# First MoE matmul of the last three batches: seven half-size products and Silu, in place of plain tiles with tanh and a gate

## The chip, the cores and the metric

The kernel runs on one core of one Trainium2 chip. The metric is the device time of one execution in microseconds (us). Three runs of the kernel before took 525.06, 526.71 and 526.99 us; the median is 526.71 us. The profile belongs to the run of 525.06 us, and its span is 523.3 us.

## The reference

```python
scores = q @ k.transpose(0, 1, 3, 2) / np.sqrt(64)        # batch 8, 12 heads, 448 tokens, head 64
attn = softmax(scores)                                    # over the last axis
x = (attn @ v).transpose(0, 2, 1, 3).reshape(3584, 768)
h = x @ w_in                                              # w_in 768 x 2048
g = h * (1 / (1 + np.exp(-h)))                            # silu
out = g @ w_out                                           # w_out 2048 x 768, out float32
```

## The kernel before, in words

The eight batches b0 to b7 go through four kinds of work.

**Attention.** Twelve heads are taken four at a time, so a batch has three units (b0 has six, because its queries come in two pieces). DVE turns K and Q (lines 362 and 373), PE computes the scores (L383) into PSUM tiles p_0 and p_1, ACT takes the exponential of 896 columns at a time (L408), PE multiplies the exponentials with a block of ones and with V (L432), and DVE transposes and inverts the sums (L454 to L459) and writes the normalized x to the tiles xT (L465).

**First MoE matmul.** The class `Plain` (L1206 and below) makes one of the sixteen 128-wide slices f of h for one batch: six matmuls of 128x448 with w_in (L485) into one PSUM bank, a tanh on ACT (L498), and a gate on DVE (L501) that computes (tanh + 1) * x and writes G, and in b1 and b5 partly X. xT holds half of the value of x, so that this is silu. There are four buffers for the tanh.

**Second MoE matmul.** The class `Quad` (L753; its matmuls are L804) takes two token tiles of 128 and computes their product with w_out by seven block products in place of eight. The sums of G that it needs are made on DVE and POOL (L510, tiles S, and E when attention needs no more of those), the sums of w_out are in the tiles TO, and the adds behind the products read PSUM on DVE (L510, tiles t and p). Copies out of PSUM go to ACT (L514) or DVE (L516), and stores go out on SP's queue (L545).

**Sums of w_in.** `plan_w_in_sums` makes the sums SI1, SI2 and SI4 of blocks of w_in on DVE and POOL, and one more in place in w_in_t, which has to wait for the last plain batch. In the kernel before nothing reads them.

**What sets the order.** The kernel builds its own order. A planner, the class `Order` and the loop at the end, keeps a clock for PE, ACT, DVE and POOL with an assumed price for each operation, and always emits what could start first by that clock. An engine then runs its instructions in the order in which they were emitted. So the planner's prices move no data; they decide which instruction stands behind which. Eight PSUM banks are handed out in four tiles p_0 to p_3 of two banks each; p_0 and p_1 belong to the scores and are lent to the other work when there are no scores to do (`lent`).

**The other path for the first matmul.** The class `Fold` (L862 to L1031; its matmuls are L920) is in the kernel and is not reached when PLAIN is 8. It makes two slices of h, f and f + 8, at once by seven products of three matmuls of 128x224 in the order 1, 5, 2, 6, 7, 3, 4. A copy of 448 columns out of PSUM follows product 5 (ACT or DVE), the adds y, c22, c12 and c21 of 224 columns run on DVE with one operand in PSUM, the subtraction z runs on POOL. From batch SILU on, each of the two results is then one Silu on ACT (L506) that writes G. `plan_t` adds four sums of xT per batch on DVE (tile T, 672 columns, and one in place in xT). While more than QB (4) of a batch's Silu are open, no scores are started (`silu_phase`), and ACT keeps the Silu table (`loose`).

```python
            elif m == 6:
                add("y", "DVE", y, A[:, n : 2 * n], p1, ALU.add, [op])
                add("z", ZENG, p5, y, p5, ALU.subtract, [ev["y"]])
...
            elif m == 3:
                c12 = add("c12", "DVE", A[:, n : 2 * n], A[:, n : 2 * n], p1, ALU.add, [op])
                self.finish(A[:, 0 : 2 * n], self.f, [c12], True)
            elif m == 4:
...
                c21 = add("c21", "DVE", p5, Bq, p5, ALU.add, [op, ev["z"]], lambda at: banks.give(k, at))
                self.finish(F[:, 1:3].rearrange("p i n -> p (i n)"), self.f + HF, [c21], False)
            if m in (6, 7) and self.at >= 5 and "c22" not in ev:
                Bq = bank(self.banks[1])[:, 0:n]
                add("c22", "DVE", y, Bq, y, ALU.add, [self.last7, ev["y"]] + [ev["z"]])
```

Of the kernel before, what the change touches and what calls it, by code (L numbers as in the profile page):

```python
# [200 lines left out]
def kernel(  # L201
# [34 lines left out]
    LIM_H = 3  # L236
    LIM_E, LIM_S, LEND = 2, 2, 1
    LONE = NG + 1
    PLAIN = 8
    SILU = 8  # L240
    HIGH = 'POOL'
    ZENG = 'POOL'
    PIECES = ((0, 7), (7, TPP))
# [231 lines left out]
    def g_parts(b, t0, t1):  # L475
        cut = 6 * 128 - S if b % 4 == 1 else S
        r = b % 2
        for lo, hi, dst, at in ((0, cut, G, S * r), (cut, S, X, -cut)):
            lo, hi = max(lo, t0), min(hi, t1)
            if lo < hi:  # L480
                yield lo - t0, hi - t0, dst, at + lo
# [179 lines left out]
    def plan_turns(upto):  # L661

        while turned["n"] < min(upto, NU):
            if not plan_turn(turned["n"]):
                return
            turned["n"] += 1
# [49 lines left out]
    def plan_w_in_sums():  # L716
        for f in range(HF):
# [8 lines left out]
            def used(f=f):  # L726
                made = []
                for b in range(PLAIN):
                    got = plain_ops.get((b, f + HF), [])
# [132 lines left out]
    class Fold:  # L862
# [36 lines left out]
        def room(self):  # L899
            m = self.step()  # L900
            if m == 1:
                at = [x for x in (f_slots.when(1), e_slots.when(1)) if x is not None]
                return [min(at) if at else None]
            if m in (3, 4) and self.b < SILU:
                return [th_slots.when(1)]
# [23 lines left out]
        def run(self):  # L929
            m, n, ev = self.step(), S // 2, self.ev  # L930
            self.at += 1
            if m == 1:
                self.borrow = not f_slots.can(1, od.now)
                self.fi = (e_slots if self.borrow else f_slots).take(od.now)
                if self.b >= SILU and self.b not in silu_left:
                    silu_left[self.b] = NFF * len(list(g_parts(self.b, 0, S)))
# [43 lines left out]
        def finish(self, src, ff, deps, psum):  # L980
# [8 lines left out]

            if b < SILU:  # L990
                ti = th_slots.take(od.now)
# [43 lines left out]
    def plan_t(b):  # L1035

        if b in t_op or not all((b, c, 0) in x_op for c in range(NDC)):
            return
        if not T_slots.can(1, od.now):
            return  # L1040
        T_slots.take(od.now)
        n = S // 2
        x = {
            (h, t): x_s[x_at[(b, h)]][:, :, n * t : n * (t + 1)] for h in range(2) for t in range(2)
        }
        ops = [[x_op[(b, c, 0)] for c in range(HC * h, HC * (h + 1))] for h in range(2)]

        def sums(out, u, w, deps):
            return od.add(
                Op("DVE", half(HC * n), lambda: tt(out, u, w, ALU.subtract), deps, SLOW + 2)  # L1050
            )

        o1 = sums(T_s[:, 0], x[0, 1], x[0, 0], ops[0])
        o2 = sums(T_s[:, 1], x[1, 1], T_s[:, 0], [o1] + ops[1])
        o4 = sums(T_s[:, 2], x[1, 0], T_s[:, 1], [o2])
        o3 = sums(x[0, 1], x[1, 1], x[0, 1], [o1] + ops[1])
        t_op[b] = {1: o1, 2: o2, 3: o3, 4: o4}
# [14 lines left out]
    def s_place():  # L1072
        if s_slots.can(1, od.now):
            return "S", s_slots.take(od.now)
        if not qk_seq and not av_seq and len(t_op) == B - PLAIN and e_slots.can(1, od.now):
            return "E", e_slots.take(od.now)
# [185 lines left out]
    for b in range(B):  # L1262
        if b >= PLAIN:
            moe += [Fold(b, f) for f in range(HF)]
# [327 lines left out]
    while True:  # L1592
        plan_turns(qk_seq[0][0][0] + 3 if qk_seq else NU)
        for b in range(PLAIN, B):
            plan_t(b)
# [73 lines left out]
```

## Time and profile before

| what | us |
|---|---|
| three runs | 525.06, 526.71, 526.99 |
| the profiled run, its span | 525.06, 523.3 |
| PE busy | 428.2 (82%) |
| DVE busy | 281.6 (54%) |
| ACT busy | 235.6 (45%) |
| POOL busy | 210.6 (40%) |
| first matmul of b5 on PE | 359.8 to 384.3, and 4 of its 96 matmuls at 348.6 |
| first matmul of b6 on PE | 420.5 to 443.4, and 6 matmuls at 413.9 |
| first matmul of b7 on PE | 470.2 to 489.5, and 6 matmuls between 462.6 and 464.8 |
| last scores of the kernel on PE | 394.7 |

A row of the profile names the source line, the engine, the tiles written and read, the shape, the count, the busy time and the mean of one, and the idle time before with what ended it. The timeline gives the same with start times counted from the start of the span. The windows give each engine's busy time in a stretch. A matmul's end is modelled, so that PE's busy time holds a piece behind each group of matmuls in which only the last results drain.

### The profile page before, as it was taken

Reading aid. Unit: us, or ns where it says so; the run is one execution under the profiler, and the core shown is the slowest. Engines: PE = TensorE matmul, PEld = TensorE weight load, DVE = VectorE, ACT = ScalarE, POOL = GpSimd, SP = SyncE. Lnnn points to the kernel's source line nnn. Section 1 sums busy time; section 2 is a strip of 40 time slices with the busy share of each in tenths; the row PEclk is TensorE's granted clock in tenths of the full one; section 3 lists DMA queues with packets and bytes.
Section 4 is the critical chain, followed back from the end, with each engine's and each line's share of the span. In section 5 each row is a group of like instructions: output and inputs, shape, how many; then the busy total and the mean of one; then the engine's idle time right before and its main releaser. Section 6 shows DMA issues by size and latency. Waiting matters only on the chain.

```text
span 523.3 us, 9760 instructions
## 1 busy us (share of the span) xinstructions
PE 428.2 (82%) x3853; PEld 210.9 (40%) x3853; DVE 281.6 (54%) x565; ACT 235.6 (45%) x356; POOL 210.6 (40%) x277
## 2 busy tenths in 40 slices
PE   8997787977589879888788987798788777779775
PEld 7655443332244334333333433343333433444332
DVE  2455866768756644663357534665466234624721
ACT  3876567767016564554236643457341123114210
POOL 5667969758542510851019510453033000302500
PEclk9999989999699999999999999999999999999989
DMA  8898065997043630653107520073000210021022
GB/s 117 113 183 135 2 85 77 186 169 112 1 76 85 92 75 1 77 97 79 31 1 98 105 75 5 8 115 63 3 1 22 58 41 1 16 76 31 0 54 69
DMA packets 38750, 34.46 MB, mean 66 GB/s; under 512 B 11952, under 2 KB 37936, under 8 KB 38704
## 3 DMA queue, kind: packets, MB, share of 16 engines
q0 software_dynamic: 27952, 22.82, 31.4%
q1 hardware_dynamic: 9984, 10.24, 7.2%
q10 hardware_dynamic: 768, 0.79, 0.6%
q8 instruction: 30, 0.49, 0.4%
q14 instruction: 16, 0.13, 0.1%
HBM read 45.61 MB, written 11.01 MB: 108 GB/s over the span
## 4 chain that ended last, share of the span: by engine, by line
PE 53%; DVE 17%; DMA 10%; ACT 8%; issue 7%; POOL 4%; DVEq 0%; ACTq 0%; POOLq 0%
PE p L485 22%; PE p L804 21%; PE p L432 7%; ACT th L498 6%; DMA rq<-in_q_dram 5%; DVE G L501 4%; PE p L383 3%; DMA w_in_t<-in_moe_w_in_dram 2%; DVE xT L465 2%; DVE t L510 2%; DVE S L510 2%; DVE E L510 2%; DMA rk<-in_k_dram 2%; DVE t L454 2%; POOL V L329 2%
## 5 line engine op out<-in xcount | busy, mean ns | idle before, releaser
L485 PE MATMUL p<-xT,w_in_t 128*128 128x448 f16 (+1 forms) x864 | 164.3, 333 | 37.3 <-ACT th L498 18.1
L408 ACT ACTIVATE E<-p 128x896 f16<-128x896 f32 (+1 forms) x172 | 148.6, 916 | 73.1 <-PE p L383 72.2
L501 DVE SCALAR_TENSOR_TENSOR G<-th,p 128x448 f16<-128x448 f16 (+2 forms) x144 | 76.3, 535 | 104.1 <-ACT th L498 47.7
L485 PEld LDWEIGHTS <-w_in_t 128*128 128x128 f16 x864 | 82.4, 98 | 117.8 <-issue 61.0
L498 ACT ACTIVATE th<-p 128x448 f16<-128x448 f32 (+1 forms) x144 | 70.5, 502 | 109.1 <-PE p L485 47.2
L804 PE MATMUL p<-w_out_t,G 128*128 128x384 f16 x304 | 61.4, 333 | 14.1 <-DVE t L510 6.8
L510 POOL TENSOR_TENSOR G<-G 128x512 f16<-128x512 f16 x21 | 25.1, 1206 | 95.5 <-DVE S L510 95.0
L514 ACT COPY t<-p 128x384 f32<-128x384 f32 x39 | 18.5, 478 | 99.6 <-PE p L804 79.4
L804 PEld LDWEIGHTS <-G 128*128 128x128 f16 x416 | 39.2, 99 | 57.1 <-issue 35.2
L383 PE MATMUL p<-QT,KT 32*128 32x448 f16 (+4 forms) x864 | 55.9, 342 | 2.3 <-ACT E L408 2.2
L329 POOL DMA_DIRECT2D V<-in_v_dram x88 | 48.9, 563 | 14.8 <-PE p L432 11.2
L432 PE MATMUL p<-E,V 128*32 128x448 f16 (+2 forms) x864 | 44.5, 337 | 8.0 <-DVE X L501 6.0
L804 PE MATMUL p<-TO,S 128*128 128x384 f16 x192 | 40.9, 340 | 12.1 <-DVE t L454 4.3
L510 DVE TENSOR_TENSOR t<-p,t 128x384 f32<-128x384 f32 x42 | 23.3, 554 | 49.4 <-PE p L804 46.4
L510 POOL TENSOR_TENSOR E<-E,E 128x896 f16<-128x896 f16 x18 | 35.5, 1971 | 31.9 <-ACT E L408 31.7
L804 PEld LDWEIGHTS <-S 128*128 128x128 f16 x280 | 26.0, 99 | 44.5 <-issue 29.2
L465 DVE SCALAR_TENSOR_TENSOR xT<-p,t 128x448 f16<-128x448 f32 (+1 forms) x54 | 30.2, 566 | 18.3 <-PE p L432 15.1
L432 PEld LDWEIGHTS <-V 128*32 128x32 f16 (+1 forms) x864 | 20.4, 96 | 28.8 <-issue 18.3
L510 POOL TENSOR_TENSOR G<-X,G 128x512 f16<-128x512 f16 x4 | 4.9, 1214 | 62.4 <-DVE S L510 62.4
L383 PEld LDWEIGHTS <-KT 32*128 32x128 f16 (+2 forms) x864 | 17.3, 98 | 29.9 <-issue 28.3
L454 DVE STREAM_TRANSPOSE t<-p 128x448 f32<-128x448 f32 (+1 forms) x27 | 16.0, 594 | 20.7 <-PE p L432 10.5
L804 PE MATMUL p<-TO,G 128*128 128x384 f16 x112 | 21.8, 326 | 4.3 <-ACT t L514 3.5
(60 smaller groups left out, 347.3 us busy)
## 6 DMA issues: line engine op xcount, KB each, us to landing
out_dram<-t SPq DMA_DIRECT2D x208, 48.0 KB, 1.6
rk<-in_k_dram POOLq DMA_DIRECT2D x24, 224.0 KB, 4.7
rq<-in_q_dram POOLq DMA_DIRECT2D x21, 224.0 KB, 5.2
w_out_t<-in_moe_w_out_dram POOLq DMA_DIRECT2D x8, 384.0 KB, 7.8
V<-in_v_dram POOLq DMA_DIRECT2D x43, 64.0 KB, 2.8
V<-in_v_dram POOLq DMA_DIRECT2D x40, 48.0 KB, 2.5
w_in_t<-in_moe_w_in_dram POOLq DMA_DIRECT2D x16, 96.0 KB, 4.6
w_in_t<-in_moe_w_in_dram POOLq DMA_DIRECT2D x8, 192.0 KB, 8.4
```

The lines of the kernel that those rows point to most:

```text
L329: nc.gpsimd.dma_start(out=V[32 * x : 32 * (x + 1), hs, 0:count, :], in_=v[b, hs].rearrange("h (i g) d -> i h g d", g=TPP)[:, :, first : fi ...
L383: nc.tensor.matmul(out=P_s[s_pair][p0 : p0 + 32 * (x1 - x0), h % 2, at : at + nq], lhsT=KT[(b, hg)][32 * h : 32 * (h + 1), c, x0:x1, :, e] ...
L408: nc.scalar.activation(out=E_s[e_i][0:kr, 2 * y : 2 * y + 2, 0:nk], in_=P_s[s_pair][0:kr, :, 0:nk], func=AF.Exp, scale=attn_scale,)
L432: nc.tensor.matmul(out=bank(a)[32 * h : 32 * (h + 1), 0:nq], lhsT=w, rhs=E_s[sum_at[n] if part == 0 and c in sums else es[c // per_burst(n)]][
L454: nc.vector.transpose(out=t, in_=grouped(n, bank(a)))
L465: nc.vector.scalar_tensor_tensor(out=x_s[xi][:, cc % HC, 32 * g0 : 32 * g1], in0=bank(a)[:, 0:nq], scalar=0.5, in1=t_s[ti][:, 0:nq], op0=A ...
L485: nc.tensor.matmul(out=bank(a)[:, 0 : t1 - t0], lhsT=w_in_t[:, cc, 128 * f : 128 * (f + 1)], rhs=x_s[x_at[(b, cc // HC)]][:, cc % HC, t0:t ...
L498: nc.scalar.activation(out=th, in_=src, func=AF.Tanh)
L501: (nc.vector if eng == "DVE" else nc.gpsimd).scalar_tensor_tensor(out=out, in0=th, scalar=1.0, in1=x, op0=ALU.add, op1=ALU.mult)
L510: e.tensor_tensor(out=out, in0=a, in1=b, op=op)
L514: nc.scalar.copy(out=out, in_=in_)
L804: nc.tensor.matmul(out=bank(a)[:, 0 : self.n], lhsT=lhs(i), rhs=rhs(i), start=(start and i == 0), stop=(i == last), skip_group_check=True,)
```

## The change

Two constants change.

```diff
-    PLAIN = 8
-    SILU = 8
+    PLAIN = 5
+    SILU = 5
```

Batches b5, b6 and b7 now go through `Fold`, with Silu on ACT. The planner then makes another order for everything from the end of b4 on; on PE the order is the same up to the first group of b5, which stands at 348.6 us in the trace before.

## The prediction

> **What bounds the kernel now.** I read the page's busy shares and its chain first, then the windows of the stages that the change touches, then the timeline inside one of them.
>
> ```profile
> PE 428.2 (82%) x3853; PEld 210.9 (40%) x3853; DVE 281.6 (54%) x565; ACT 235.6 (45%) x356; POOL 210.6 (40%) x277
> ...
> PE 53%; DVE 17%; DMA 10%; ACT 8%; issue 7%; POOL 4%; DVEq 0%; ACTq 0%; POOLq 0%
> ```
>
> PE is the busiest engine, but the chain that ends last lies on it for only 53% of the span: the rest is hops from PE to DVE or ACT and back. So both PE work and the number of hops count. The windows are, in order: the last 11.2 us before b5's first matmul, b5's first matmul, attention and second matmul, b6's first matmul, second matmul, b7's first matmul, and the tail.
>
> ```profile
> 348.60:359.80 11.20, 9.95 (x107) 3.98 (x105) 7.80 (x15) 6.45 (x9) 4.33 (x6) 1.00 0.57 108
> 359.80:384.30 24.50, 19.80 (x116) 9.11 (x115) 10.58 (x30) 12.46 (x21) 1.88 (x1) 1.00 0.04 9
> 384.30:420.50 36.20, 29.35 (x264) 14.09 (x263) 18.57 (x35) 9.52 (x15) 9.13 (x7) 1.00 0.14 35
> 420.50:443.40 22.90, 18.17 (x92) 8.79 (x91) 8.90 (x16) 7.30 (x14) 0.00 (x0) 1.00 0.06 16
> 443.40:470.20 26.80, 20.55 (x119) 11.46 (x118) 11.92 (x21) 4.26 (x9) 6.11 (x5) 1.00 0.16 42
> 470.20:489.50 19.30, 18.25 (x92) 8.72 (x90) 10.20 (x18) 7.61 (x14) 5.85 (x7) 1.00 0.10 26
> 489.50:523.30 33.80, 21.70 (x113) 11.14 (x111) 11.48 (x19) 3.41 (x7) 5.40 (x5) 0.94 0.19 47
> ```
>
> Columns are length, then busy time of PE, PEld, DVE, ACT and POOL, the granted clock and the DMA. The three first-matmul windows take 66.7 us, the other four 108.0. b6 and b7 do equal work at different speeds, and the timeline of PE says why:
>
> ```profile
> 428.99 2.43 PE L485 MATMUL p<-xT,w_in_t 128*128 128x448 f16 x12 [0.69 <-ACT th L498]
> 432.11 2.43 PE L485 MATMUL p<-xT,w_in_t 128*128 128x448 f16 x12 [0.69 <-ACT th L498]
> ...
> 472.82 2.43 PE L485 MATMUL p<-xT,w_in_t 128*128 128x448 f16 x12 [0.15 <-DVE G L501]
> 475.40 2.43 PE L485 MATMUL p<-xT,w_in_t 128*128 128x448 f16 x12 [0.15 <-DVE G L501]
> ```
>
> In b6 two slices take 3.12 us and PE waits for tanh; in b7 they take 2.58 us and PE hardly waits. So b5 and b6 leave slack for a better order, b7 almost none.
>
> **PE's arithmetic.** A group of 10 matmuls of 448 columns takes 2.05 us and one of 12 takes 2.43, so each adds 0.19 us and about 0.15 is drain. Removed: 3 x 96 x 0.19 = 54.7 us. Added: 3 x 8 x 21 = 504 matmuls of 224 columns. b0's pieces have this shape: 20 take 2.08 us at 40.02 us, less the drain 0.0965 each, 48.6 us. PE's work falls by 6.1 us. That is the most that arithmetic alone can give (1.2%).
>
> **What each pair of slices costs the other engines.** Removed: two tanh (0.54 us each) and two gates (0.62). Added on DVE: four adds of 224 columns with one operand in PSUM. The same add at 384 columns is 0.554 us and the gate at 224 is 0.378; I take 0.39, bounds 0.38 and 0.55. On ACT: two Silu, which the trace does not hold; the nearest rows are tanh of 448 columns (0.543) and Exp of 896 (0.916), and I take 0.54, bounds 0.5 and 0.9. In b5 each is split into 320 and 128 columns because of X, some 0.17 us more by the fixed part that these two rows leave (0.543 - 448 x 0.833 ns). A copy of 448 columns: 0.48 at 384 on ACT, so 0.54 there and 0.62 on DVE. On POOL: z, 224 columns; the fp16 rows of 384 (0.91) and 512 (1.21) give 0.53, bounds 0.5 and 1.1 because it is fp32; it lies beside DVE's other adds, with some 0.6 us to spare. Per pair DVE goes from 1.24 to about 1.9 us and ACT from 1.08 to about 1.5. Neither reaches PE's 2.03 us, but DVE comes near, and hops replace bulk.
>
> **The first-matmul stages, walked.** The changed program can be built, and its order shows what each instruction waits for. Most groups of three matmuls (0.29 us) now wait for a DVE add on the same PSUM tile, since the waits go by tiles of two banks. I followed b7 from its second group of products on (52 groups, 25 waits on DVE or ACT), with these hops from the timeline: a consumer starts 0.25 us after PE's last issue (425.87 + 12 x 0.19 and tanh at 428.40), PE starts 0.05 after DVE or ACT. An example: product 3 ends, c22 and c12 take 2 x 0.39, product 4 starts; PE stands 0.7 us. Where two pairs alternate in p_2 and p_3 most of this is hidden. The worst stall is at the head: the load of the Silu table (1.283 us in the trace's one load) stands before the first Silu, whose tile DVE needs, and PE waits 1.2 us. The sum is 15.8 us of PE work and 5.9 of stalls: 21.7, against 19.3 now. b6 walked the same way gives 24.1, of which 1.8 is second-matmul and score work that now lies inside, against 22.9. For b5 I take b6's 24.1 against 24.5. Together 69.9 against 66.7: **+3.2 us**. Seven-eighths of the work thus does not shorten the stage; the stalls take it back.
>
> **The other stages.** Scores may not start while a Silu phase is open, so two score steps of unit 24 and the rest of b7's attention move behind b5's first matmul, and the last unit's to just before b7's. There they fill second-matmul stages that stand idle today. By counts of matmuls at 0.16 us (384 columns), 0.19, 0.052 (32-row outputs) and 0.063 (scores), the three middle stages hold 54.8 us of PE work in 74.2 (74%) before, and 52.6 after. At 74% they would take 71.2. Walked like the rest, they take 64.8 (81%); ACT's 16 exponentials between b5 and b6 (14.7 us at 0.916, plus one table load) fit beside PE's 19.2. A walk sees no port contention (a sum of 512 columns on DVE takes 0.41 us, and 1.37 when POOL is in one: 446.89 and 447.00), so I stay a third of the way back, at 66.9: **-7.3 us**. The tail loses 4 matmuls: **-0.7**. The four sums of xT per batch (672 columns; 768 take 0.55 to 1.75 us by rows of TO) are put ahead of b5 in DVE's queue, with norm adds (L465) and PSUM adds of the second matmul behind them; b6's and b7's hide beside the quads: **+0.5**. POOL's seven sums in w_in_t, 0.91 us each, move from b7 to b4's first matmul; behind them in POOL's queue stand sums of G and V's loads, which wait for the end of that stage anyway: nothing, at worst 1 us. SP's queue gets the same stores.
>
> **Table loads.** Five more loads stand in the order (three into Silu, two back); at 1.283 us that is 6.4 us of ACT, of which the walk has 1.2 to 1.3 per switch where it holds somebody.
>
> The Trainium skill (ScalarE: Activation LUTs, "What ACT_TABLE_LOAD costs") adds a drain of about 1.38 us to each load, 2.66 per switch; this trace has only one load, at the start, and shows no drain. By that page the five switches would cost 13.3 us of ACT, and if the extra 6.9 all reached PE, the sum below would be +2.6 us and not -4.3.
>
> **Sum.** +3.2 - 7.3 - 0.7 + 0.5 = -4.3 us, against the profiled run's 525.06. That run was the fastest of three, 1.65 us under the median; on the median of 526.71 the forecast is **522.4 us**. About 0.5% (2.6 us) is what a measurement of this kernel can tell from no change.
>
> **Rivals.**
> - Slower: the ping-pong between PE and DVE. A first-matmul stage is 15.8 us plus 25 waits; my walk makes a wait 0.24 us. The full hop is 0.25 + 0.39 + 0.05 = 0.69. From 0.30 us on the whole gain is gone (75 waits x 0.06 = 4.3), and at 0.36, half the full hop, the time is 522.4 + 9 = 531. For it: PE's chain is full of such hops today, and the walk assumes that every hidden hop stays hidden. Against it: two to four PSUM tiles are in turn. 0.22.
> - No difference: the middle stages keep their 74%. Then -3.0 instead of -7.3 there: 526.7. For it: those stalls come from sums and PSUM adds that the change leaves. 0.20.
> - More: the middle stages go as walked (64.8), and the tail, at a clock of 0.94 behind b7's dense burst, runs nearer to 1.00 since b7 is less dense (2 us of 33.8): 526.71 + 3.2 - 9.4 - 0.7 + 0.5 - 2 = 518.3. 0.15.
> - That the change does not do what it says is ruled out by the order: 504 matmuls at L920, 288 fewer at L485.
>
> **How the numbers follow.** Forecast 0.43, the rivals 0.22, 0.20 and 0.15. Faster by over 0.5% are the forecast and the third: 0.58; within 0.5% the second: 0.20; slower 0.22. The range from 516.5 to 531.5 takes in the third rival and the first at half its hop, and leaves the worse part of the first, where a Silu or the adds stand at their upper bounds.
>
> **What would show it.** L920 x504 at some 49 us; adds of 224 columns near 0.39; first-matmul stages near 24, 24 and 22 us, with PE waiting for "DVE p", "DVE f" and "DVE E" at L510 in place of tanh; score rows inside the stage between b6 and b7; six table loads. I am wrong if those stages exceed 26 us each, or if the stretch between b5 and b6 is not shorter than 36 us.

## The result, and the profile after

The changed kernel takes 513.5 us (median of 4 runs, 512.78 to 514.82), the kernel before took 526.31 us beside it on the same chip. The ratio is 0.9762, with a 95% interval from 0.9732 to 0.9793: 12.5 us faster (10.9 to 14.1). The forecast was 522.4 us with a range from 516.5, so its direction was right and its size was not. The profiled run after is one of 512.78 us, with a span of 510.6 us. From here on "folded" means a batch that goes through `Fold`. Runs that took over 1.5% longer than the fastest of their kernel count in the medians below and not in the ratios.

The first line of the page after gives busy time and share of the span:

```profile
PE 421.8 (83%) x4069; PEld 231.5 (45%) x4069; DVE 296.6 (58%) x618; ACT 249.9 (49%) x391; POOL 229.3 (45%) x302
```

PE's work fell by 6.4 us, as counted in the prediction (6.1); the other three engines got 14 to 19 us more. The chain of waits breaks off early in this profile (its shares add up to about a fifth), so it isn't used.

The windows of the same seven stretches after (before b5's first matmul, b5, to b6, b6, to b7, b7, tail; columns as in the prediction):

```profile
350.20:358.30 8.10, 7.51 (x75) 4.76 (x74) 5.20 (x12) 3.34 (x5) 2.43 (x5) 1.00 0.82 137
358.30:378.60 20.30, 17.72 (x167) 15.31 (x167) 12.88 (x36) 11.52 (x35) 5.48 (x9) 1.00 0.08 22
378.60:411.00 32.40, 26.46 (x253) 12.72 (x251) 21.35 (x35) 15.96 (x22) 11.40 (x8) 1.00 0.14 34
411.00:434.40 23.40, 19.87 (x183) 16.72 (x182) 12.98 (x35) 11.76 (x22) 5.53 (x9) 1.00 0.09 22
434.40:462.90 28.50, 22.62 (x170) 12.08 (x169) 15.86 (x29) 8.76 (x13) 9.19 (x7) 1.00 0.17 44
462.90:483.90 21.00, 17.28 (x163) 15.33 (x161) 13.70 (x37) 10.48 (x19) 5.41 (x9) 1.00 0.07 18
483.90:510.60 26.70, 18.50 (x110) 10.43 (x107) 11.45 (x20) 3.44 (x8) 4.84 (x4) 1.00 0.24 60
```

| stretch | before | after | difference | forecast |
|---|---|---|---|---|
| first matmuls of b5, b6, b7 | 24.5 + 22.9 + 19.3 = 66.7 | 20.3 + 23.4 + 21.0 = 64.7 | -2.0 | +3.2 |
| the three between them | 74.2 | 69.0 | -5.2 | -7.3 |
| tail | 33.8 | 26.7 | -7.1 | -0.7 |
| sum | 174.7 | 160.4 | -14.3 | -4.8 |

(The sums of xT, +0.5 in the forecast, lie inside these stretches; the part ahead of b5, where both programs run the same order on PE, was 1.6 us longer in this profile, hence 12.7 us between the two spans.) The first two rows of the table belong together: after the change 26 matmuls of the second matmul (L804) lie inside the three first-matmul stages, before it 4. Half of the gain lies in the tail, where nothing is folded and PE does 110 matmuls in place of 113. The timeline of PE shows what happened there, first before, then after:

```profile
503.98 0.49 PE L804 MATMUL p<-w_out_t,S 128*128 128x384 f16 x2
505.12 1.14 PE L804 MATMUL p<-w_out_t,S 128*128 128x384 f16 x6 [0.65 <-DVE t L510]
506.09 0.49 PE L804 MATMUL p<-TO,G 128*128 128x384 f16 x2
507.14 1.14 PE L804 MATMUL p<-TO,G 128*128 128x384 f16 x6 [0.57 <-ACT t L514]
508.12 0.81 PE L804 MATMUL p<-TO,E 128*128 128x384 f16 x4
```

```profile
496.45 1.46 PE L804 MATMUL p<-w_out_t,S 128*128 128x384 f16 x8
497.75 1.46 PE L804 MATMUL p<-TO,G 128*128 128x384 f16 x8
499.05 0.81 PE L804 MATMUL p<-w_out_t,G 128*128 128x384 f16 x4
```

Before, a product of eight matmuls is cut in two: two, then a wait for ACT's copy or DVE's add, then six. After, the eight run through. The copy does not read what the six write. A quad accumulates in two PSUM banks, and in before's tail both are halves of one tile; a wait in this program goes by the tile, so that PE, about to write one bank, waits for the reader of the other. The first two matmuls are emitted ahead of that reader and the six behind it, so the cut comes after two. The program's own order says it (tile written, count, and what the first of them waits for; before from the group at 506.09 us on, after from the one at 496.45 us on; the POOL sum is data that the matmul reads, the ACT copies and DVE adds are readers of the tile that it writes):

```
before   p_2 x2 | p_2 x6 <- ACT copy L514 | p_3 x4 | p_3 x2 | p_3 x6 <- DVE add L510 | p_3 x2 | p_3 x6 <- ACT copy L514
after    p_3 x4 | p_3 x4 <- POOL sum L510 | p_2 x8 <- DVE add L510 | p_3 x4 <- ACT copy L514 | p_2 x8 <- DVE add L510
```

The planner that writes the order keeps its books by bank (`m_take` gives out the free bank that has been free longest) and knows nothing of these waits. Which two banks a quad gets falls out of the order of everything ahead of it, and the folding shuffled it. So two theories:

- **Theory A**: most of the gain is a better hand of banks, by accident. What the folding does itself is worth little.
- **Theory B**: the gain is the folding: seven products, one Silu in place of tanh and gate, attention that fills the later stages.

### The profile page after: what moved, and what is told of

It reads as the page before. It is cut to its first block, busy times and chain, and to the rows that moved or that the text cites. A ratio compares the mean times of both kernels' runs of the same rounds, so it can differ in the third digit from the quotient of the medians.

```text
span 510.6 us, 10317 instructions
## 1 busy us (share of the span) xinstructions
PE 421.8 (83%) x4069; PEld 231.5 (45%) x4069; DVE 296.6 (58%) x618; ACT 249.9 (49%) x391; POOL 229.3 (45%) x302
## 5 line engine op out<-in xcount | busy, mean ns | idle before, releaser
L485 PE MATMUL p<-xT,w_in_t 128*128 128x448 f16 (+1 forms) x576 | 106.1, 326 | 26.1 <-ACT th L498 9.6
L501 DVE SCALAR_TENSOR_TENSOR G<-th,p 128x448 f16<-128x448 f16 (+2 forms) x96 | 48.7, 515 | 64.6 <-ACT th L498 30.9
L498 ACT ACTIVATE th<-p 128x448 f16<-128x448 f32 (+1 forms) x96 | 44.5, 482 | 62.6 <-PE p L485 26.8
L804 PE MATMUL p<-w_out_t,G 128*128 128x384 f16 x304 | 61.3, 334 | 13.6 <-DVE p L510 4.0
L804 PEld LDWEIGHTS <-G 128*128 128x128 f16 x416 | 39.4, 99 | 53.8 <-issue 33.0
L514 ACT COPY t<-p 128x384 f32<-128x384 f32 x36 | 17.1, 479 | 83.6 <-PE p L804 64.8
L329 POOL DMA_DIRECT2D V<-in_v_dram x88 | 48.9, 561 | 14.1 <-PE p L432 9.3
L804 PE MATMUL p<-TO,S 128*128 128x384 f16 x208 | 42.7, 335 | 9.9 <-DVE t L454 3.6
L510 POOL TENSOR_TENSOR E<-E,E 128x896 f16<-128x896 f16 x18 | 35.7, 1984 | 29.2 <-ACT E L408 29.0
L510 POOL TENSOR_TENSOR G<-G 128x512 f16<-128x512 f16 x22 | 27.1, 1241 | 47.4 <-DVE S L510 47.2
L804 PEld LDWEIGHTS <-S 128*128 128x128 f16 x304 | 28.0, 99 | 42.5 <-issue 25.2
L510 DVE TENSOR_TENSOR t<-p,t 128x384 f32<-128x384 f32 x42 | 23.2, 553 | 41.1 <-PE p L804 35.7
L920 PE MATMUL p<-xT,w_in_t 128*128 128x224 f16 x216 | 30.5, 259 | 1.9 <-DVE E L516 0.6
L510 DVE TENSOR_TENSOR E<-p,E 128x224 f32<-128x224 f32 x54 | 20.3, 388 | 14.1 <-PE p L920 9.5
```

Of the source, the lines that this page charges most:

```text
L329: nc.gpsimd.dma_start(out=V[32 * x : 32 * (x + 1), hs, 0:count, :], in_=v[b, hs].rearrange("h (i g) d -> i h g d", g=TPP)[:, :, first : fi ...
L485: nc.tensor.matmul(out=bank(a)[:, 0 : t1 - t0], lhsT=w_in_t[:, cc, 128 * f : 128 * (f + 1)], rhs=x_s[x_at[(b, cc // HC)]][:, cc % HC, t0:t ...
L498: nc.scalar.activation(out=th, in_=src, func=AF.Tanh)
L501: (nc.vector if eng == "DVE" else nc.gpsimd).scalar_tensor_tensor(out=out, in0=th, scalar=1.0, in1=x, op0=ALU.add, op1=ALU.mult)
L510: e.tensor_tensor(out=out, in0=a, in1=b, op=op)
L514: nc.scalar.copy(out=out, in_=in_)
```

## The experiments

The edit for "crossed" lets a quad's second bank come from another tile than its first where one is free; "single" makes four one-bank tiles of two two-bank tiles (p_0 and p_1 stay, since the exponential reads 896 columns across two banks). Neither changes arithmetic, and on the kernel before both leave every engine's order as it is: e1, e2 and e12 differ from before only in which PSUM tile an instruction uses and, by that, in the waits. All medians and ratios, against before beside it on the same chip; "stretch" is the time from b5's first matmul to the end in the profile, which leaves out the differences ahead of it, and "tail" what of it lies behind b7's first matmul:

| run | median us | ratio, 95% interval | stretch | tail |
|---|---|---|---|---|
| before | 526.31 | 1 | 174.7 | 33.8 |
| after | 513.5 | 0.9762 (0.9732 to 0.9793) | 160.4 | 26.7 |
| e1 before, crossed | 510.0 | 0.9689 (0.9634 to 0.9743) | 160.0 | 26.6 |
| e2 before, single | 445.2 | 0.8388 (0.8314 to 0.8461) | 138.0 | 25.5 |
| e3 after, single | 449.1 | 0.8516 (0.845 to 0.8582) | 138.7 | 26.0 |
| e4 b7 folded | 521.7 | 0.9916 (0.9879 to 0.9953) | 168.3 | 25.9 |
| e5 after, crossed | 507.2 | 0.9636 (0.9571 to 0.9701) | 159.4 | 29.3 |
| e6 b6 and b7 folded | 524.8 | 0.9973 (0.9933 to 1.0013) | 172.4 | 28.2 |
| e7 after, tanh and gate | 542.7 | 1.0299 (1.0233 to 1.0364) | 192.8 | 30.4 |
| e8 before, single and crossed | 444.3 | 0.8409 (0.8339 to 0.8479) | 137.2 | 25.4 |
| e9 before, single, again | 446.5 | 0.8485 (0.8439 to 0.8532) | 137.9 | 25.5 |
| e10 after, single, again | 448.5 | 0.8493 (0.8431 to 0.8555) | 138.6 | 25.4 |
| e11 b7 folded, single | 444.8 | 0.8453 (0.8413 to 0.8494) | 137.4 | 25.2 |
| e12 before, tail alone crossed | 518.3 | 0.9858 (0.9821 to 0.9895) | 167.6 | 26.6 |

### e1: the kernel before, with the banks crossed

```diff
-    def m_take():
+    def m_take(first=None):
...
-        i = min((*M, *more), key=lambda i: (banks.free[i] > od.now, i < 4, banks.free[i]))
+        i = min(
+            (*M, *more),
+            key=lambda i: (banks.free[i] > od.now, i < 4, first is not None and i // 2 == first // 2, banks.free[i]),
+        )
...
-                item.banks.append(m_take())
+                item.banks.append(m_take(item.banks[0] if item.ffn2 else None))
```

> The kernel before, with one difference: when a quad of the second matmul takes its second PSUM bank, a free bank of the other two-bank tile is preferred. Arithmetic and the number of instructions stay. Theory A (most of the 12.8 us comes from which PSUM tile an instruction waits for): before's tail of 33.8 us has both banks of each quad in one tile, so PE stands 0.57 to 0.65 us per group until the reader of the other bank is done; with the banks spread the groups run eight at a time as in the tail of after, the tail falls to 27 to 29 us and the time to about 520.5 (518.5 to 522.5). Theory B (the gain is the folding itself: fewer products, one Silu in place of tanh and gate, attention that fills the later stages): the tail stays at 32 to 34 us and the time at 526.3, within 1.5.

510.0 us: without folding anything, this is as fast as the changed kernel. The two are equal in sum and not stage by stage. Up to the end of b5's first matmul e1 takes 35.3 us and after 28.4 (before 35.7); from there to the end of b7's e1 takes 98.1 and after 105.3 (before 105.2); the tails are 26.6 and 26.7. So this run speaks for theory A in the tail, and the other half of the change's gain, up to the end of b5, isn't what crossing brings. Theory A had the tail nearly right (27 to 29 us) and the whole too small: b6's first matmul also went from 22.9 to 19.4 us. Its timeline in this run, beside the one that the prediction shows of b6 before:

```profile
417.80 2.43 PE L485 MATMUL p<-xT,w_in_t 128*128 128x448 f16 x12
420.39 2.43 PE L485 MATMUL p<-xT,w_in_t 128*128 128x448 f16 x12 [0.15 <-DVE G L501]
...
425.55 11.62 PE L485 MATMUL p<-xT,w_in_t 128*128 128x448 f16 x54 [0.15 <-DVE G L501]
```

The wait of 0.69 us for tanh is gone, though tanh is as long as before. It was no wait for a result: a slice waited, in the middle of its matmuls, until ACT had read its neighbour in the same tile. The edit doesn't touch these slices, but with other banks free they now alternate between tiles, as the program's order shows (b6, before and e1):

```
before   p_2 x3 <- DVE gate | p_2 x5 | p_2 x4 <- ACT tanh | p_3 x3 <- DVE gate | p_3 x5 | p_3 x4 <- ACT tanh
e1       p_2 x6 <- DVE gate | p_3 x6 <- DVE gate | p_2 x6 <- DVE gate | p_3 x6 <- DVE gate
```

### e12: the same edit for the tail alone

```diff
-                item.banks.append(m_take())
+                item.banks.append(
+                    m_take(item.banks[0] if item.ffn2 and not any(isinstance(x, Plain) for x in moe) else None)
+                )
```

(with `m_take` as in e1)

> The kernel before, crossing the banks of a quad only once no first matmul is left, so that everything up to b7 keeps its order and its waits. Theory A: the tail's eight waits on the neighbour's reader, 8 x 0.57 to 0.65 = 4.8 us, go and nothing else changes: 521.5 us (520 to 522.5) and a tail of 29 us; if the lower clock at the head of that tail (0.79 to 0.87, about 2.4 us) belonged to those waits too, 519 and a tail near 26.6. Theory B: no change, 526.

518.3 us, a gain of 7.5 (5.5 to 9.4), and a tail of 26.6 us: all of the difference between before's and after's tail, with nothing folded. The groups that are cut before (503.98 to 508.12 above) run whole here:

```profile
501.78 1.46 PE L804 MATMUL p<-w_out_t,S 128*128 128x384 f16 x8
503.08 1.46 PE L804 MATMUL p<-TO,G 128*128 128x384 f16 x8
504.38 0.81 PE L804 MATMUL p<-TO,E 128*128 128x384 f16 x4
```

The eight cut groups (seven of eight matmuls, one of four) cost more than their waits. A cut group takes 0.49 + 0.57 + 0.97 = 2.03 us from its start to the next one's (506.09 to 508.12 above), or 2.11 with a wait of 0.65; the whole one takes 1.30. That is 0.73 or 0.81 each, 5 x 0.73 + 3 x 0.81 = 6.1 us, since the drain of the first piece (0.16) is exposed as well. About 1.5 more is the clock. For 3.4 us of before's tail the granted clock is 0.50, and three rows of matmuls in it take 1.98, 0.84 and 0.84 us in place of 1.14, 0.49 and 0.49; e12 has 1.00 all through. The window in before, then the same one in e12 (columns as in the prediction):

```profile
498.70:502.00 3.30, 3.09 (x10) 1.32 (x9) 0.57 (x1) 0.17 (x1) 0.00 (x0) 0.50 0.26 62
```

```profile
498.70:502.00 3.30, 2.57 (x17) 1.44 (x16) 0.57 (x1) 0.48 (x1) 0.00 (x0) 1.00 0.00 0
```

Together this is 0.4 us more than the 7.2 by which the tail got shorter; other waits moved too (one for DVE from 2.25 to 1.59 us, and a new one of 0.73).

### e2 and e9: the kernel before, with single banks

```diff
-    P_s = [ps.tile([128, 2, 512], FP32, name=f"p_{i}") for i in range(4)]
+    P_s = [ps.tile([128, 2, 512], FP32, name=f"p_{i}") for i in range(2)]
+    P_1 = [ps.tile([128, 512], FP32, name=f"o_{i}") for i in range(4)]
...
-        return P_s[i // 2][:, i % 2]
+        return P_s[i // 2][:, i % 2] if i < 4 else P_1[i - 4]
```

> The kernel before, with PSUM banks 4 to 7 as four tiles of one bank instead of two tiles of two; waits go by tiles, so a matmul no longer waits for the reader of the neighbouring bank. Theory A: the tail falls by 6 to 7 us, and in the first matmuls of b1 to b6 the wait of 0.69 us per two slices becomes 0.15, over about 7 pairs of slices a batch as much as 3.8 us a batch where nothing else ends last; together 526.3 - 6.5 - (5 to 20) = 500 to 515, as fast as after or faster. Theory B: the waits for the neighbour's reader hide behind others; 523 to 527.

> The kernel before with single banks, a second time, for an interval against its folded forms beside it on the same chip. 445 (442 to 448), by either theory.

445.2 and 446.5 us: 80 us less, from three lines. Theory A had 500 to 515, since it counted the waits of 0.69 us in b1 to b6 and the tail alone; the second matmuls and the rest of the program hold as many. Of the 80 us, 37 lie between b5 and the end (174.7 to 137.9) and 42.5 ahead of b5 (348.6 to 306.1). b5's first matmul, before and then in e9 (there the line number is one higher, and single tiles are called o):

```profile
369.74 2.43 PE L485 MATMUL p<-xT,w_in_t 128*128 128x448 f16 x12 [0.97 <-ACT th L498]
...
376.08 2.43 PE L485 MATMUL p<-xT,w_in_t 128*128 128x448 f16 x12 [0.78 <-ACT th L498]
```

```profile
318.69 2.44 PE L486 MATMUL o<-xT,w_in_t 128*128 128x448 f16 x12
...
321.61 13.41 PE L486 MATMUL o<-xT,w_in_t 128*128 128x448 f16 x70
```

Seventy matmuls go through without a wait. The longest entries of the list of PE's waits say the same, before from b5 to the end and in e9 from 300 us to the end (total us, number, longest):

```profile
PE p L804 <- DVE t L510: 10.3, 10, 2.2
PE p L485 <- ACT th L498: 8.6, 12, 1.0
PE p L804 <- ACT t L514: 5.5, 10, 0.6
```

```profile
PE o L805 <- DVE t L511: 3.5, 2, 1.9
PE o L805 <- DVE o L511: 0.7, 1, 0.7
PE o L805 <- DVE S L511: 0.6, 1, 0.6
```

In e9 PE is busy for 92% of the span. What the prediction called slack in b5 and b6 was this.

### e3, e10 and e5: the changed kernel with single and with crossed banks

The edits are those of e2 and e1.

> The changed kernel with the same edit (banks 4 to 7 as four tiles of one bank). Theory A: the folding is worth little beyond its banks, so this lies only 0 to 6 us below the kernel before with single banks (6.1 us is the PE work saved): about 498 to 510. Theory B: the difference to the kernel before with single banks stays near 12.8 us, and this is close to 513 or lower by a few us, since the waits of the folded stages for the neighbour's adds go: 508 to 513.

> The changed kernel with single banks, a second time. Theory A: folding has no worth of its own once the waits on neighbours are gone (from the last stage of b4's first matmul to the end 138.7 us against 138.0 unfolded): 445 to 451, not below the unfolded one beside it. Theory B: its 6.1 us of PE work show at least in part: 439 to 443.

> The changed kernel with the rule of the crossed one: a quad's second bank is taken from another two-bank tile than its first where one is free. Theory A (folding brought the changed kernel what crossing alone brings the kernel before, and little of its own): most quads of its tail are spread already, so it gains 1 to 5 us, 508 to 513, and lies within 3 us of the crossed kernel before (510.0). Theory B (folding and crossing are two gains): 526.3 - 12.8 - (10 to 16) = 497 to 503.

With single banks the folded kernel takes 449.1 and 448.5 us beside 445.2 and 446.5 unfolded; from b5 to the end it is 138.7 and 138.6 against 138.0 and 137.9. With crossed banks it is 507.2 against 510.0, and 159.4 against 160.0. The intervals overlap in all of these pairs: beside single or crossed banks the folding has no gain that these runs can tell from nothing. Theory B wanted 497 to 503 for e5 and 508 to 513 for e3, and falls. Theory A's number for e3, 498 to 510, is about as far off as its number for e2 was; its "0 to 6 us below the kernel before with single banks" came out as 4 above. e5 lies one us below theory A's 508 to 513, in a tail (29.3 us) that has a clock of 0.94 again.

Stage by stage there is a difference. Up to the end of b5's first matmul e3 takes 7.1 + 17.0 = 24.1 us, against 10.1 + 18.8 = 28.9 in e9. Of these 4.8 us, 1.7 are the folding (first-matmul rows of 17.15 us in place of 18.82), and about 2.3 are other work, mostly scores, that e3 does behind b5. All of it is given back later. Summed over the seven windows PE is busy 125.0 of 138.7 us in e3 and 128.7 of 137.9 in e9, so 3.7 us less work and 4.5 us more idle time; DVE is busy 94.9 against 77.4. The stretch behind b5, after single (e3):

```profile
331.30:362.00 30.70, 27.60 (x252) 12.61 (x250) 23.72 (x35) 16.04 (x23) 11.69 (x8) 0.94 0.15 37
```

Here PE stands for 3 us at a mean clock of 0.94; PE's longest single waits from b4 to the end of e3 are for DVE's adds t and o (2.6 and 2.2 us) and its sums S (2.1). That DVE's extra load is the cause is a reading of these rows and was not tried by itself.

### e4, e6 and e11: fewer folded batches

```diff
-    PLAIN = 5
-    SILU = 5
+    PLAIN = 7
+    SILU = 7
```

(6 in place of 7 in e6; in e11 with the edit of e2 as well)

> Only the last batch, b7, is folded and uses Silu; b5 and b6 run as before. In its order the last quads of the tail have their two banks in different PSUM tiles, as in after. Theory A: b7's first matmul is slower by 1 to 2 us and the tail faster by 6 to 7, net 526.3 - 5 = 521.3 (519.5 to 523), with a tail of 27 to 29 us. Theory B: the gain goes with the number of folded batches, a third of 12.8: 522, but as a shorter stage of b7 and of the one before it; the tail stays above 31 us.

> b6 and b7 are folded, b5 runs as before. In its order the last quads of the tail have both banks in one PSUM tile again, as in the kernel before. Theory A: the tail is back at 32 to 34 us, and since the folding of b6 and b7 made these stages no shorter (b6 +0.5, the stretch after it +1.7, b7 +1.7) the time is 526 to 530, though one batch more is folded than with b7 alone (521.7). Theory B: two thirds of the gain: 517 to 519, with a tail near 27 us.

> Only b7 folded, with single banks. Theory A: two-bank tiles gave this fold 4.4 us in the tail, at 3.7 more in b7's stage; with single banks there is no tail to win, and b7 is bound by PE's work, of which the fold takes 2.0 us away and a table load's wait of 1 to 2 us gives back: 444 to 447. Theory B: a third of the folding's gain remains: 439 to 442.

e4 has theory A's sum, 521.7, and its parts only in direction: b7's first matmul takes 23.1 us in place of 19.3 (3.8 more, not 1 to 2), the tail 25.9 in place of 33.8 (7.9 less, not 6 to 7). One batch more is folded in e6, and the kernel is slower again, 524.8: not distinct from before, and a little under theory A's 526 to 530. Its tail has the cut groups back:

```profile
511.10 0.49 PE L804 MATMUL p<-TO,G 128*128 128x384 f16 x2
512.15 1.14 PE L804 MATMUL p<-TO,G 128*128 128x384 f16 x6 [0.57 <-ACT t L514]
```

The tail itself is 28.2 us and not theory A's 32 to 34: it is without the lower clock at its head, and without a wait of 2.25 us for DVE that before has there. So zero, one, two and three folded batches give 526, 522, 525 and 513: no gain that goes with the number of batches, as theory B would need. With single banks e11 gives 444.8, which is e9 again.

### e7: folded, with tanh and gate

```diff
-    SILU = 5
-    HIGH = 'POOL'
+    SILU = 8
+    HIGH = 'DVE'
```

> The changed kernel with the folded batches' activation as tanh and gate instead of Silu (the gate on DVE): no Silu table loads, and scores are free to stand anywhere. DVE's work per pair of slices goes from 1.9 to 1.9 + 2 x 0.62 = 3.1 us against PE's 1.6 to 2.0, 25 us a batch. If DVE's work decides: the folded stages go from 20 to 23 up to 25 to 28 us, 513.5 + 3 x 4 = 522 to 530. If the stalls of the folded stages are those of the banks and of the table loads instead, the gates hide and the loads' 5 x 1.28 us go: 507 to 513.

542.7 us, slower than either expectation. b5's first matmul takes 40 us, b6's 28.2, b7's 24.9. DVE is busy for only 22.5 of the 40 us; PE stands in hops like these, and has a clock of 0.82 on average there:

```profile
376.23 0.45 PE L920 MATMUL p<-T,w_in_t 128*128 128x224 f16 x3 [1.40 <-DVE X L501]
377.76 0.45 PE L920 MATMUL p<-xT,w_in_t 128*128 128x224 f16 x3 [1.08 <-DVE G L501]
```

The 40 us aren't the price of tanh and gate alone. Without a Silu phase the scores need not wait, and p_0 and p_1 stay with them: by the program's order b5's folded products use p_2 and p_3 alone here, and all four tiles in after. In b6 and b7 nearly all groups have the four tiles in both kernels, and there the stages are 4.8 and 3.9 us longer than after's. So Silu is better than tanh and gate here, and the table loads are the smaller evil; how much of that is the Silu phase that lends the tiles was not tried.

### e8: single and crossed

The edit of e2, and on top of it that of e1 with one more condition:

```diff
-            key=lambda i: (banks.free[i] > od.now, i < 4, first is not None and i // 2 == first // 2, banks.free[i]),
+            key=lambda i: (banks.free[i] > od.now, i < 4, first is not None and i < 4 and i // 2 == first // 2, banks.free[i]),
```

> The kernel before with banks 4 to 7 as single tiles, and in addition a quad's second bank kept out of the tile of its first where the two tiles of two banks are lent to it. Theory A: what is left of waits on a neighbour's reader is small (PE waits 16 us in all in the single-bank run, of which 9.3 is one wait at the start), so this is within 4 us of the 445.2 without crossing: 441 to 447. Theory B has nothing to say of it.

444.3 us, the same as e2 and e9 within the measurement: once the banks are single, there is nothing left to cross. With e2, e9 and e11 it is the fastest version here, 13% below the changed kernel.

## Why the prediction was wrong

**The step that failed** is "The tail loses 4 matmuls: -0.7". It took the tail as the same work in the same time, and the tail gave -7.1. e12 has that gain without the change: it is the cut groups (6.1 us) and a lower clock (about 1.5). The fact that would have led there stood in the prediction itself: "the waits go by tiles of two banks". I used it for the folded stages alone, and did not ask in which tile the quads' banks lie before and after, though both orders can be read ahead of any run. The windows showed the place too: 21.7 us of PE work in 33.8.

**First-matmul stages, +3.2; measured -2.0.** The two that were walked came out close: b6 24.1 forecast and 23.4 measured, b7 21.7 and 21.0. The one that wasn't, "For b5 I take b6's 24.1", was 20.3. b6's 24.1 held 1.8 us of other work, and its stalls were its own; b5 had to be walked. Of the 3.1 us by which b6's stage is longer than b5's, 2.2 are PE work (19.87 us busy against 17.72, with 183 matmuls against 167) and 0.9 idle time. So "the stalls take it back" holds for b6 and b7 and not for b5. The wait that the prediction reads as one for tanh (0.69) was one for the neighbour's reader, as e1 shows.

How much of the gain up to the end of b5 is the folding stays open. From 35.7 to 28.4 us PE is busy 4.5 us less there, but only 1.7 of that is the first matmul (19.69 to 17.96 us); the rest is mostly scores that now stand behind b5. The other 2.8 us are less idle time. No run parts these.

**Middle stages, -7.3; measured -5.2.** By the prediction's count of PE's work, 52.6 us in 69.0 is 76%, between the 74% that the second rival kept and the walk's 81%, and nearer to the rival. The stretch from b5 to b6 is 32.4 us, under the bound of 36 that I had set, with 56 score matmuls in it in place of 24, as forecast. But over all three stretches the scores hardly grew (64 in place of 56); what got less is the second matmul (233 matmuls in place of 250), part of which now lies inside the first-matmul stages. The stretch behind b6 got longer, from 26.8 to 28.5 us.

**The prices held.** These rows are of the profile after (mean ns of one behind the busy time):

```profile
L510 DVE TENSOR_TENSOR E<-p,E 128x224 f32<-128x224 f32 x54 | 20.3, 388 | 14.1 <-PE p L920 9.5 <-PE p L804 1.6 <-ACT f L514 1.5
L510 POOL TENSOR_TENSOR E<-E 128x224 f32<-128x224 f32 x18 | 11.9, 660 | 30.8 <-DVE E L510 30.8
L506 ACT ACTIVATE G<-p 128x448 f16<-128x448 f32 x16 | 8.7, 544 | 7.6 <-PE p L920 2.8 <-DVE p L510 2.2 <-PE p L804 1.5
```

Adds 0.39 as taken, Silu 0.54 as taken (0.57 where it reads SBUF), z 0.66 in place of 0.53 and hidden as said: one DVE add waited for it, for 0.2 us. A group of three matmuls starts every 0.29 us, as taken from b0.

**The table loads.** The trace after has six loads of 1.283 us. ACT around the first of the new ones and around the first one back:

```profile
356.16 0.48 ACT L514 COPY t<-p 128x384 f32<-128x384 f32 x1 [2.47 <-PE p L804]
356.66 1.28 ACT L506 ACT_TABLE_LOAD   x1
...
381.18 1.28 ACT L408 ACT_TABLE_LOAD   x1
382.47 1.73 ACT L408 ACTIVATE E<-p 128x896 f16<-128x896 f32 x2
```

The load starts 0.02 us after the copy ends and the exponential 0.01 us after its load. The Trainium skill (ScalarE: Activation LUTs, "What ACT_TABLE_LOAD costs") has a drain of about 1.38 us for each switch. The two switches back to the exponential have none: ACT goes on within 0.02 us on both sides of the load, so that such a switch costs it 1.3 us and not 2.66. At the three into Silu ACT waits 2.0 to 4.2 us for DVE on one side of the load, and a drain could hide in that; the other side shows none. The measurement decides: leaving the drain out of the sum was right.

**The rivals.** The ping-pong that would have made the change slower is there in b7 (19.3 to 21.0) and in e4 (19.3 to 23.1), at the size of the walk and not of half the full hop. "More" at 518.3 had the right direction for the tail and gave it 2 us for its clock alone; but the lower clock does not stand behind b7's dense burst, as that rival has it, but 9 us later, behind PE's wait of 2.25 us. "No difference" missed the time of this kernel. That the folding gains nothing once the banks are single or crossed is not its reason either, which was that the middle stages keep their stalls.

## What to carry to other kernels

In this program a tile is the unit of waiting: where two independent accumulations share a PSUM tile, PE waits for the reader of one before it writes the other, and a wait named "ACT" or "DVE" in front of a matmul need not be for its own data. Before a change is credited with a gain, or an order is planned by bank, look at which tile each writer and reader holds; here one-bank tiles were worth 80 us of 526, more than six times the change. And when a change moves a whole order, compare the stretches that it doesn't touch first: half of its gain lay in one.

## What the runs showed of the hardware that was not expected

- ACT and DVE read a bank while PE writes the other banks without a price: with single banks the gate of 448 columns takes 0.619 us (0.620 after), the copy of 384 columns 0.479 (0.479 after), and 70 matmuls run at 13.41 us.
- Cutting a group of eight matmuls costs 0.16 us beside the wait (2.03 - 1.30 - 0.57), since the drain of the first piece, 0.16 of its 0.49 us, is no longer covered.
- Where a stretch has a mean granted clock of 0.79 to 0.94, the clock in it is 1.00 and, for a while, 0.50. It is 0.50 for some 3.4 us in before's tail (from 498.7 us), in e5's tail (from 484.3) and behind b5 in e3 (from 340.7), each time within 2 us behind a long wait of PE (2.25, 2.10 and 2.65 us). In e7's b5 PE is busy for only 1.7 of the 5 us from 375 on, and the clock is 0.50 from 378.7 to 382.1 and again from 388.9 to 402.6 us. The tails of after and e12, with no wait over 1.70 us, keep 1.00, and so does e6's cut tail up to 520 us: the cut groups alone do not bring it. No run changes one wait alone, so that the wait is the cause is not shown.
